# Logits of eight units at a time, one key scaling moved to VectorE, and the last unit's logits with its result as the stationary operand

## The chip, the cores and the metric

One core of one Trainium2 chip runs the whole program as one launch. The metric is device time in microseconds (us), the median of a few runs. The engines are named as in the profile: PE is TensorE (PEld its weight load), DVE is VectorE, ACT is ScalarE, POOL is GpSimd, SP is the engine that issues most of the loads and stores.

## The reference

First comes a gated linear attention, token by token, for 4 batches of 8 heads, 768 tokens, head size 48:

```
state = alpha[:, :, t, :, None] * state + einsum('bhd,bhe->bhde', k[:, :, t], v[:, :, t])
y[:, :, t] = einsum('bhd,bhde->bhe', q[:, :, t], state)
```

Its output, seen as 3072 rows of 384 channels, goes through a mixture of 8 experts. The logits are `x @ w_gate`. All 24,576 pairs of token and expert are gone through in order of falling logit; a token goes to the first expert that has fewer than 384 tokens so far. Each expert then computes `relu(x @ w1) @ w2` on its 384 tokens.

## The kernel before

**Attention.** The work is cut into 24 units, n = 0 to 23: unit n is 128 tokens (chunk n // 4) of batch n % 4, with all 8 heads. For each unit, `unit(n)` records these steps:
- DVE: a backward scan of the decay, `sc` (line 449), a reciprocal (451), a forward scan `ga` (454), and, for 18 of the units, the key scaling `kh` (459).
- POOL: the query scaling `qh` (464), the causal mask on the scores `sm` (502, two halves), and for the units in `K_POOL` the key scaling instead of DVE.
- PE: keys turned (485), scores `s` (495), states (510), and the result `y`, first the part carried from the state, then the part within the chunk (both 541).
- ACT: copies of these out of the PSUM, among them `yta` (564), the unit's result, channels on the partitions.
- DVE: the new state `st` (526), for units 0 to 19 from the second chunk on.

**Logits.** `logits(g, ns)` computes a group of units in `LOGITS`. PE multiplies the gate weights (stationary, 32 columns per unit) with the units' results (574). A unit's logits stand in one of four partition blocks, so four units fill a tile. ACT copies the tile (600), PE turns it (585), and DVE copies it into the table `L` (591). The last unit has a group of its own: four partial products side by side (582), which DVE sums (589) after the same copy and turn.

**Choice and routing.** When the first 20 units' logits are in `L`, DVE computes their digit tables (`choice(0, ...)`); the last four units follow in `choice(1, ...)`, which starts with the maximum on line 621. Then a search over digits alternates between DVE compares (935) and PE counts (906, 882) and gives the token list of the first expert. The attention result must stand in DRAM by then, tokens on the rows, since the tokens are gathered from there: each unit is turned by PE (four pieces, line 692 or 701), copied by ACT and stored by SP (710). `Y_EARLY` = 4 units are turned during attention, units 4 to `Y_IN_ATTENTION` - 1 at its end, the rest between the steps of the search.

**Experts.** 8 experts of 30 us follow, nearly all PE. Constants for the routing (line 331 to 413) are made on POOL between the attention's steps.

**What sets the order.** Every step is recorded by `op(...)` with an engine, an estimated duration, what it reads and writes, and a due time `at`. `plan()` simulates the engines and emits the instructions of each engine in the order that results; each engine then runs its own list in order. So a change of one step can move others on every engine. `banks` names PSUM areas that two engines shall not use at the same moment: the logits' tile and the states' tile share the areas `T` and `KX`.

Of the kernel before, what the change touches and what calls it, by code (L numbers as in the profile page):

```python
# [15 lines left out]
WARM_UP = 10  # L16
Y_IN_ATTENTION, Y_EARLY, EARLY_AT = 10, 4, 3.0
CUTS, CUTS_L = (0, 16, 24), (0, 12, 20, 24)
SAME, CHOICE, AHEAD_S = 0.8, 23.15, 0.8
LOGITS = ((0, 4), (4, 8), (8, 12), (12, 16), (16, 20), (20, 23), (23, 24))  # L20
CONST_AT, CONST_STEP, FILLS, FILL_END = 2.5, 0.5, 80, 6
FIRST_DMA = (dict(al=-0.4, k=0.87, q=1.35, v=0.5), dict(al=0.66, k=1.02, q=0.68, v=0.65))
WG_AT, Q_DVE, K0_AT = -1.4, (), 0.05
K_FIRST = ()
K_ELSE, K_POOL, M_ACT = 0, {n: 4 for n in (2, 6, 10, 14, 18, 22, 23)}, range(4, 23)
F0, TE = 26.0, 30.5
# [11 lines left out]
AF = mybir.ActivationFunctionType  # L38
OP = mybir.AluOpType
# [3 lines left out]
def gla_moe_kernel(ctx, tc, q, k, v, alpha, w_gate, w12, out):  # L43
    nc = tc.nc
    C = 128
    NC = 6
    H = 8
    HP = H // 2
    NU = q.shape[0]
# [4 lines left out]
    E = w_gate.shape[1]  # L54
# [103 lines left out]
    def ring(name, n, shape, dtype=F32):  # L158
        return [ap_.tile(shape, dtype, name=f"{name}{i}") for i in range(n)]
# [13 lines left out]
    ST = ring("st", NBAT, [128, HP, D])  # L173
    LT = ring("lt", RING["lt"], [128, C])
    YT = [YTA[:, n].rearrange("p (h s t) -> p h s t", h=2, s=2) for n in range(NU)]
# [11 lines left out]
    kvp = kx[:, KT:KT + HP * D].rearrange("p (u d) -> p u d", d=D)  # L187
    ltp = XB[:, KT:KT + C]
    lgp = XB[:, KT + C:KT + 2 * C].rearrange("p (n e) -> p n e", e=32)
    fcp = kx[:, KT + HP * D:KT + HP * D + E]  # L190
# [378 lines left out]
    def logits(g, ns):  # L569
        def some(n0, n1):  # L570
            for j in range(HP):
                for n in range(n0, n1):
                    u = n - ns[0]
                    P_.matmul(ltp[32 * u:32 * u + 32], wg[:, j], YT[n][:, j % 2, j // 2], start=j == 0,
                              stop=j == HP - 1, skip_group_check=True)

        one = len(ns) == 1
        lt_, lg_ = (yps[:, 0, :C], yps[:, 1, :C].rearrange("p (n e) -> p n e", e=32)) if one else (ltp, lgp)

        def single():  # L580
            for j in range(HP):
                P_.matmul(lt_[32 * j:32 * j + 32], wg[:, j], YT[ns[0]][:, j % 2, j // 2], start=True, stop=True)

        def turned():
            P_.transpose(lg_.rearrange("p n e -> p (n e)"), lt, ident)

        def out_():
            if len(ns) == 1:
                V.tensor_reduce(L[:, ns[0]], lg_[:, :, :E].rearrange("p j e -> p e j"), axis=X_, op=OP.add)
            else:  # L590
                V.tensor_copy(L[:, ns[0]:ns[-1] + 1], lgp[:, :len(ns), :E])

        lt = LT[g % RING["lt"]]
        at = ns[-1]
        t_, g_ = (("Y0",), ("Y1",)) if one else (("T", "KX"),) * 2
        LT_ = "LT1" if one else "LT"
        op("PE", 0.33 if one else 0.9, single if one else lambda: some(ns[0], ns[-1] + 1), shape=32,
           r=[("yt", n) for n in ns] + [("wg", 0)], w=[(LT_, g)], banks=t_, at=at + 1.0,
           after=lastw["yt", NU - 2] if one else ())
        op("ACT", 0.3, lambda: A.activation(lt, lt_, AF.Copy), r=[(LT_, g)], w=[("lt", g)], banks=t_, at=at + 1.0)  # L600
        op("PE", 0.12, turned, shape=128, r=[("lt", g)], w=[("LG", g)], banks=g_, at=at + 1.1,
           after=() if one else lg_read[-1:])
        lg_read.append(op("DVE", 0.18, out_, r=[("LG", g)], banks=g_, at=ns[-1] + 1.1, after=copied[-1:]))
        copied.append(lg_read[-1])

# [811 lines left out]
```

## Time and profile before

| | us |
|---|---|
| median of 3 runs (lowest, highest) | 370.01 (369.34, 370.06) |
| the profiled execution, whole | 369.01 |
| its span, first to last instruction | 367.4 |
| PE busy | 350.3 (95%) |
| DVE busy | 267.0 (73%) |
| ACT busy | 185.8 (51%) |
| POOL busy | 177.9 (48%) |

The granted clock of PE is 0.991 of full speed over the span. The shares are means over stages with different limits: POOL is idle for long in the experts' part and nearly full in attention. Attention takes the first 97 us, the search and the first gather the next 20, the experts the rest.

### The profile page before, as it was taken

The numbers are of one execution on the slowest core, as the hardware profiler recorded it, in microseconds if no ns is written. First come the engines' busy times: TensorE is split into PE (matmuls) and PEld (weight loads), VectorE is DVE, ScalarE is ACT, GpSimd is POOL, SyncE is SP. The second block draws the span as 40 slices with busy tenths as digits, with TensorE's granted clock in tenths as the row PEclk, the third lists the DMA queues.
The fourth block names the chain that finished last, engine by engine and source line by source line (L and its number), as shares of the span: only waits on it lengthen the run. The fifth ranks groups of instructions, "written<-read, shape, count | busy, mean of one in ns | idle before, by whom it ended". The sixth has DMA issues, their size and how long they took to land.

```text
span 367.4 us, 9669 instructions
## 1 busy us (share of the span) xinstructions
PE 350.3 (95%) x3710; PEld 310.8 (85%) x3710; DVE 267.0 (73%) x741; ACT 185.8 (51%) x387; POOL 177.9 (48%) x298
## 2 busy tenths in 40 slices
PE   8989999999999999899999999999999999999990
PEld 4778888887776779789899989889989999999990
DVE  7999999998878998888978978878777733131110
ACT  4697888886551741651552553543462474343120
POOL 2898999999402312351524625603722862304021
PEclk9999999999999999999999999999999999999996
DMA  7999998840176956999799699698898899986001
GB/s 232 368 351 377 394 300 265 272 131 2 45 249 221 324 105 167 306 173 271 245 218 260 206 243 237 206 272 165 277 266 171 297 337 239 287 201 127 24 22 43
DMA packets 28782, 81.71 MB, mean 222 GB/s; under 512 B 3904, under 2 KB 10304, under 8 KB 28736
## 3 DMA queue, kind: packets, MB, share of 16 engines
q0 software_dynamic: 11024, 52.70, 54.2%
q1 hardware_dynamic: 17712, 28.39, 22.7%
q8 instruction: 29, 0.48, 0.5%
q14 instruction: 17, 0.14, 0.1%
HBM read 71.64 MB, written 9.44 MB: 221 GB/s over the span
## 4 chain that ended last, share of the span: by engine, by line
PE 61%; DVE 19%; issue 9%; DMA 3%; POOL 3%; SPq 1%; ACT 1%; POOLq 0%; DVEq 0%; ACTq 0%
PE h L1283 21%; PE y L1315 21%; PE y L541 3%; DVE sc L449 3%; PE xt L882 3%; PE s L495 2%; DVE ga L454 2%; PE h L1135 2%; DVE kh L459 2%; DVE wset L1190 2%; DMA al<-in_alpha_dram 2%; DVE cmp L935 1%; DMA vr<-in_v_dram 1%; POOL out_dram L1335 1%; DVE xl L1259 1%
## 5 line engine op out<-in xcount | busy, mean ns | idle before, releaser
L1315 PE MATMUL y<-wset,hh 128*128 128x384 f32 x384 | 101.7, 342 | 0.0
L1283 PE MATMUL h<-xh,wset 128*128 128x384 f32 x384 | 93.4, 345 | 0.3 <-DVE hl L1298 0.3
L1296 ACT ACTIVATE hh<-h 128x384 fp32r<-128x384 f32 x64 | 31.3, 490 | 93.7 <-PE h L1283 84.3
L1315 PEld LDWEIGHTS y<-wset,hh 128*128 128x128 f32 x384 | 69.2, 188 | 1.0 <-issue 1.0
L1283 PEld LDWEIGHTS h<-xh,wset 128*128 128x128 f32 x384 | 68.1, 188 | 0.8 <-DVE hl L1298 0.6
L1315 PE MATMUL y<-wset,hl 128*128 128x384 f32 x192 | 65.9, 343 | 0.0
L1298 DVE SCALAR_TENSOR_TENSOR hl<-h,hh 128x384 fp32r<-128x384 f32 x64 | 35.3, 554 | 39.6 <-ACT hh L1296 38.9
L1208 POOL DMA_DIRECT2D wset<-in_w_dram x23 | 20.9, 909 | 63.9 <-ACT wset L1204 63.8
L1283 PE MATMUL h<-xl,wset 128*128 128x384 f32 x192 | 47.3, 345 | 0.0
L1335 POOL DMA_INDIRECT out_dram<-yo,idx x24 | 24.9, 1039 | 41.3 <-ACT yo L1326 37.4
L1204 ACT ACTIVATE wset<-wset 128x768 fp32r<-128x768 f32 x46 | 36.6, 840 | 12.6 <-DMA wset<-in_w_dram 12.2
L1125 POOL DMA_INDIRECT xr<-x_dram,idx x24 | 25.4, 1060 | 23.5 <-DVE idx L1121 9.0
L1315 PEld LDWEIGHTS y<-wset,hl 128*128 128x128 f32 x192 | 36.1, 188 | 0.5 <-issue 0.4
L1283 PEld LDWEIGHTS h<-xl,wset 128*128 128x128 f32 x192 | 34.1, 188 | 0.9 <-issue 0.7
L502 POOL TENSOR_SCALAR_AFFINE_SELECT sm<-sm 128x512 f32<-128x512 f32 x48 | 32.2, 693 | 3.2 <-ACT sm L500 2.9
L464 POOL TENSOR_TENSOR qh<-qr,ga 128x512 f32<-128x512 f32 (+1 forms) x25 | 29.8, 1193 | 5.3 <-DVE ga L454 4.3
L454 DVE TENSOR_TENSOR_SCAN ga<-al,d 128x516 f32<-128x516 f32 (+1 forms) x25 | 29.6, 1183 | 1.8
L449 DVE TENSOR_TENSOR_SCAN sc<-al,d 128x516 f32<-128x516 f32 (+1 forms) x25 | 29.3, 1173 | 1.3 <-DMA al<-in_alpha_dram 1.2
L500 ACT ACTIVATE sm<-s 128x512 f32<-128x512 f32 x48 | 26.1, 595 | 7.3 <-PE s L495 6.8
L495 PE MATMUL s<-qh,kh 64*128 64x128 f32 x384 | 27.4, 282 | 1.0 <-POOL qh L464 1.0
L495 PEld LDWEIGHTS s<-qh,kh 64*128 64x128 f32 x384 | 23.6, 189 | 2.4 <-POOL qh L464 2.1
L1178 POOL DMA_DIRECT2D raw<-in_w_dram x9 | 5.2, 580 | 41.4 <-DVE bk L1098 19.0
(218 smaller groups left out, 590.7 us busy)
## 6 DMA issues: line engine op xcount, KB each, us to landing
wset<-in_w_dram POOLq DMA_DIRECT2D x46, 768.0 KB
raw<-in_w_dram POOLq DMA_DIRECT2D x9, 768.0 KB
qr<-in_q_dram SPq DMA_DIRECT2D x24, 256.0 KB, 4.7
kr<-in_k_dram SPq DMA_DIRECT2D x24, 256.0 KB, 4.8
al<-in_alpha_dram SPq DMA_DIRECT2D x23, 258.5 KB, 4.7
vr<-in_v_dram SPq DMA_DIRECT2D x24, 192.0 KB, 4.6
x_dram<-xga SPq DMA_DIRECT2D x8, 384.0 KB, 2.7
x_dram<-xga SPq DMA_DIRECT2D x8, 192.0 KB, 3.3
```

The costliest lines, as they stand in the source:

```text
L449: V.tensor_tensor_scan(sc[:, lo + 1:hi + 1][:, ::-1], a[:, lo + 1:hi + 1][:, ::-1], dps[:, FO + lo:FO + hi][:, ::-1], 1.0, op0=OP.mult, op ...
L454: V.tensor_tensor_scan(ga[:, lo:hi], a[:, lo:hi], dps[:, lo:hi], 1.0, op0=OP.mult, op1=OP.add)
L464: (V if n in Q_DVE else G).tensor_mul(qh[:, ps_], qr[:, ps_], ga[:, lo:hi].rearrange("p (g x) -> p g x", x=C1)[:, :, 1:])
L495: P_.matmul(sps[h][:, p], kh[hs, p], qh[hs, p], start=True, stop=True)
L500: op("ACT", 0.6, lambda h=h: A.activation(sm[:, h], sps[h], AF.Copy), r=[(f"S{h}", n)], w=[("sm", n)], banks=(f"S{h}",), at=n + 0.4)
L502: op("POOL", 0.65, lambda h=h: G.affine_select(sm[:, h], sm[:, h], pattern=[[0, HP], [1, C]], compare_op=OP.is_ge, fill=0.0, base=0, chann ...
L1204: pre.append(op("ACT", 0.84, lambda hs=hs: A.activation(WS[i % 2][:, 1, g][:, hs], WS[i % 2][:, 0, g][:, hs].bitcast(F32), AF.Copy, scale= ...
L1283: P_.matmul(o(), WS[i % 2][:, a, g, c0 + d * 128:c0 + (d + 1) * 128], x[:, d], start=m_ == 0 and d == 0, stop=m_ == 2 and d == DB - 1)
L1296: a_ = op("ACT", 0.49, lambda: A.activation(HHT[m], o(), AF.Relu), after=[y], r=[("hb", n_)], w=[("hh", n_)], at=at, boost=25, lat=0.1)
L1298: op("DVE", 0.474, lambda: V.scalar_tensor_tensor(HLT[m], o(), 0.0, HHT[m], op0=OP.max, op1=OP.subtract), after=[a_], r=[("hb", n_), ("hh" ...
L1315: P_.matmul(YB[b][:, :Dm], a[:, bs], w, start=q == 0 and n == 0, stop=q == FB - 1 and n == 2)
L1335: st_ = nc.gpsimd.indirect_dma_start(out=out, out_offset=bass.IndirectOffsetOnAxis(ap=IDX[i][:, b:b + 1], axis=0), in_=YO[c % 5], in_offse ...
```

## The change

The groups of logits become (0, 4), (4, 12), (12, 20), (20, 23), (23, 24). A group of eight units is computed as two blocks of four in one PE step; ACT copies both blocks with one instruction, PE turns them with two transposes, DVE copies both with one instruction. The group's first step now waits for the DVE copy of the group ahead of it.

The last unit's logits have the unit's result as stationary operand and the gate weights, 8 columns, as moving one. They come out with the tokens on the partitions, summed over the four channel blocks in the PSUM, and DVE copies them straight into `L`; the ACT copy, the turn and the sum go.

Unit 22 leaves `K_POOL`, so its key scaling is a DVE instruction. `Y_IN_ATTENTION` is 9, so 5 units and not 6 are turned at the end of attention, and 15 and not 14 during the search.

```diff
-Y_IN_ATTENTION, Y_EARLY, EARLY_AT = 10, 4, 3.0
+Y_IN_ATTENTION, Y_EARLY, EARLY_AT = 9, 4, 3.0
-LOGITS = ((0, 4), (4, 8), (8, 12), (12, 16), (16, 20), (20, 23), (23, 24))
+LOGITS = ((0, 4), (4, 12), (12, 20), (20, 23), (23, 24))
-K_ELSE, K_POOL, M_ACT = 0, {n: 4 for n in (2, 6, 10, 14, 18, 22, 23)}, range(4, 23)
+K_ELSE, K_POOL, M_ACT = 0, {n: 4 for n in (2, 6, 10, 14, 18, 23)}, range(4, 23)
-    LT = ring("lt", RING["lt"], [128, C])
+    LT = ring("lt", RING["lt"], [128, 2, C])
-    ltp = XB[:, KT:KT + C]
-    lgp = XB[:, KT + C:KT + 2 * C].rearrange("p (n e) -> p n e", e=32)
+    ltp = XB[:, KT:KT + 2 * C]
+    lgp = ltp.rearrange("p (n e) -> p n e", e=32)
...
         def some(n0, n1):
-            for j in range(HP):
-                for n in range(n0, n1):
-                    u = n - ns[0]
-                    P_.matmul(ltp[32 * u:32 * u + 32], wg[:, j], YT[n][:, j % 2, j // 2], start=j == 0,
-                              stop=j == HP - 1, skip_group_check=True)
+            for a in range(n0, n1, 4):
+                for j in range(HP):
+                    for n in range(a, min(a + 4, n1)):
+                        u = n - a
+                        P_.matmul(ltp[32 * u:32 * u + 32, (a - n0) // 4 * C:(a - n0) // 4 * C + C], wg[:, j],
+                                  YT[n][:, j % 2, j // 2], start=j == 0, stop=j == HP - 1, skip_group_check=True)
...
         def single():
             for j in range(HP):
-                P_.matmul(lt_[32 * j:32 * j + 32], wg[:, j], YT[ns[0]][:, j % 2, j // 2], start=True, stop=True)
+                P_.matmul(lg_, YT[ns[0]][:, j % 2, j // 2], wg[:, j, :E], start=j == 0, stop=j == HP - 1)
...
         def turned():
-            P_.transpose(lg_.rearrange("p n e -> p (n e)"), lt, ident)
+            for a in range(0, len(ns), 4):
+                P_.transpose(lg_[:, a:a + 4].rearrange("p n e -> p (n e)"), lt[:, a // 4], ident)
...
             if len(ns) == 1:
-                V.tensor_reduce(L[:, ns[0]], lg_[:, :, :E].rearrange("p j e -> p e j"), axis=X_, op=OP.add)
+                V.tensor_copy(L[:, ns[0]], lg_)
...
+        if one:
+            op("PE", 0.6, single, shape=128, r=[("yt", ns[0]), ("wg", 0)], w=[("LG1", g)], banks=("Y1",), at=at + 1.0,
+               after=lastw["yt", NU - 2])
+        else:
+            op("PE", 0.45 + 0.45 * two, lambda: some(ns[0], ns[-1] + 1), shape=32, r=[("yt", n) for n in ns] + [("wg", 0)],
+               w=[("LT", g)], banks=t_, at=at + 1.0, after=lg_read[-1:])
+            op("ACT", 0.2 + 0.1 * two, lambda: A.activation(lt[:, :two], lt_.rearrange("p (a t) -> p a t", t=C), AF.Copy),
+               r=[("LT", g)], w=[("lt", g)], banks=t_, at=at + 1.0)
+            op("PE", 0.12 * two, turned, shape=128, r=[("lt", g)], w=[("LG", g)], banks=t_, at=at + 1.1)
```

The order of the instructions moves at more places than the diff shows. On PE, in the last units of attention: before, the scores of unit 21 (`s`, from `qh0`) are followed by the logits of units 16 to 19 (16 matmuls) and the result of unit 20 (from `ms2` and `sm0`).

```order
L495 MATMUL s1_179<-qh0_161,kh0_158 128x128
L574 MATMUL xx_181<-yta_121,wg_69 32x128 x16
L541 MATMUL y_180<-qh2_163,ms2_170 48x128 x8
L541 MATMUL y_180<-sm0_166,vr2_149 48x128 x8
L585 MATMUL xx_181<-ident_63,lt0_175 128x128
L495 MATMUL s0_178<-qh1_162,kh1_159 128x128
```

The same place in the changed kernel, with the logits of units 12 to 19:

```order
L495 MATMUL s1_179<-qh0_161,kh0_158 128x128
L575 MATMUL xx_181<-yta_121,wg_69 32x128 x32
L541 MATMUL y_180<-qh2_163,ms2_170 48x128 x8
L541 MATMUL y_180<-sm0_166,vr2_149 48x128 x8
L587 MATMUL xx_181<-ident_63,lt0_175 128x128 x2
L495 MATMUL s0_178<-qh1_162,kh1_159 128x128
```

So 16 matmuls that stood four units earlier, ahead of the result of unit 16, and one transpose now stand behind the scores of unit 21. The groups (4, 8) and (8, 12) are joined in the same way at the later one's place, ahead of the scores of unit 13.

On POOL, from the query scaling of unit 20 (`qh2<-qr0`) on; `shifts_b`, `masks_b`, `scale` and `oneb4`, `oneb5` are constants for the routing. Before:

```order
L464 TENSOR_TENSOR qh2_163<-qr0_142,ga0_156 128x512
L407 MEMSET shifts_b_106 128x24
L408 MEMSET masks_b_107 128x24
L410 MEMSET scale_82 128x24
L375 MEMSET oneb5_93 128x128
L376 MEMSET oneb5_93 32x128
L502 AFFINE_SELECT sm1_167<-sm1_167 128x512 x2
L464 TENSOR_TENSOR qh0_161<-qr1_143,ga1_157 128x512
L459 TENSOR_TENSOR kh1_159<-kr2_139,sc1_154 128x512
L502 AFFINE_SELECT sm0_166<-sm0_166 128x512 x2
L464 TENSOR_TENSOR qh1_162<-qr2_144,ga0_156 128x512
```

The same stretch in the changed kernel, from the row behind the query scaling of unit 20 on:

```order
L502 AFFINE_SELECT sm1_167<-sm1_167 128x512 x2
L375 MEMSET oneb4_92 128x128
L376 MEMSET oneb4_92 32x128
L378 MEMSET oneb4_92 1x128
L407 MEMSET shifts_b_106 128x24
L408 MEMSET masks_b_107 128x24
L410 MEMSET scale_82 128x24
L464 TENSOR_TENSOR qh0_161<-qr1_143,ga1_157 128x512
L502 AFFINE_SELECT sm0_166<-sm0_166 128x512 x2
L375 MEMSET oneb5_93 128x128
L376 MEMSET oneb5_93 32x128
L464 TENSOR_TENSOR qh1_162<-qr2_144,ga0_156 128x512
```

The mask of a unit (`sm`) now follows a query scaling directly, with the constants behind it, here and at most other units; the constants `oneb5` stand behind the query scaling of unit 21 (`qh0<-qr1`), and the key scaling of unit 22 (`kh1`) is gone.

On DVE, from the state of unit 18 (`st2<-ms0`) to the scans of unit 22 and 23. Before:

```order
L526 TENSOR_TENSOR st2_173<-ms0_168,xx_181 128x192
L459 TENSOR_TENSOR kh0_158<-kr1_138,sc0_153 128x512
L449 SCALAR_TENSOR_TENSOR sc1_154<-al2_134,d_177 128x516
L451 RECIPROCAL d_177<-sc1_154 128x4
L526 TENSOR_TENSOR st3_174<-ms1_169,xx_181 128x192
L454 SCALAR_TENSOR_TENSOR ga0_156<-al2_134,d_177 128x516
L449 SCALAR_TENSOR_TENSOR sc2_155<-al3_135,d_177 128x516
```

The same stretch in the changed kernel:

```order
L526 TENSOR_TENSOR st2_173<-ms0_168,xx_181 128x192
L454 SCALAR_TENSOR_TENSOR ga1_157<-al1_133,d_177 128x516
L526 TENSOR_TENSOR st3_174<-ms1_169,xx_181 128x192
L459 TENSOR_TENSOR kh0_158<-kr1_138,sc0_153 128x512
L449 SCALAR_TENSOR_TENSOR sc1_154<-al2_134,d_177 128x516
L451 RECIPROCAL d_177<-sc1_154 128x4
L459 TENSOR_TENSOR kh1_159<-kr2_139,sc1_154 128x512
L454 SCALAR_TENSOR_TENSOR ga0_156<-al2_134,d_177 128x516
L449 SCALAR_TENSOR_TENSOR sc2_155<-al3_135,d_177 128x516
```

The key scaling of unit 22 (`kh1`) stands between the two scans of its unit, and the states of units 18 and 19 stand one place earlier, that of unit 19 ahead of the key scaling of unit 21 (`kh0`).

## Rows read from the trace of the kernel before

**Rows 1.** Busy time by stage: PE, PEld, DVE, ACT, POOL with (instructions), then PEclk, DMA share, GB/s
```profile
35.00:93.00 58.00, 57.34 (x1228) 49.02 (x1216) 53.75 (x74) 47.24 (x124) 56.34 (x114) 1.00 0.69 228
...
117.40:367.40 250.00, 237.81 (x1680) 219.82 (x1677) 162.31 (x551) 103.54 (x179) 91.74 (x126) 0.99 0.80 212
```

**Rows 2.** Waits of POOL from 35 to 93 us: us in total, times, longest
```profile
POOL qh L464 <- DVE st L526: 1.1, 1, 1.1
```

**Rows 3.** Waits of DVE from 46 to 88 us: us in total, times, longest
```profile
DVE st L526 <- PE xx L574: 1.0, 2, 0.6
```

**Rows 4.** Timeline of PE, 56 to 61 us: start us, us, instruction, count
```profile
56.42 1.12 PE L495 MATMUL s<-qh,kh 64*128 64x128 f32 x16
57.48 1.08 PE L574 MATMUL xx<-yta,wg 128*32 128x128 f32 x32
58.49 0.66 PE L541 MATMUL y<-qh,ms 48*48 48x128 f32 x16
59.07 1.08 PE L541 MATMUL y<-sm,vr 128*48 128x128 f32 x16
60.09 0.33 PE L585 MATMUL xx<-ident,lt 128*128 128x128 f32 x1
60.34 0.56 PE L510 MATMUL xx<-vr,kn 128*48 128x48 f32 x16
60.84 0.45 PE L485 MATMUL xx<-ident,kh 48*128 48x48 f32 x8
```

**Rows 5.** Timeline of PE, the scores of units 21 and 23; [idle before, releaser]
```profile
85.12 1.16 PE L495 MATMUL s<-qh,kh 64*128 64x128 f32 x16
...
92.04 1.16 PE L495 MATMUL s<-qh,kh 64*128 64x128 f32 x16 [0.21 <-POOL qh L464]
```

**Rows 6.** Timeline of POOL, 52 to 86 us
```profile
52.02 1.77 POOL L502 TENSOR_SCALAR_AFFINE_SELECT sm<-sm 128x512 f32<-128x512 f32 x2
...
58.41 1.17 POOL L464 TENSOR_TENSOR qh<-qr,ga 128x512 f32<-128x512 f32 x1
59.54 1.67 POOL L502 TENSOR_SCALAR_AFFINE_SELECT sm<-sm 128x512 f32<-128x512 f32 x2
...
74.55 1.67 POOL L502 TENSOR_SCALAR_AFFINE_SELECT sm<-sm 128x512 f32<-128x512 f32 x2
...
78.16 0.22 POOL L375 MEMSET oneb<- 128x128 bf16 x1
...
82.28 0.20 POOL L375 MEMSET oneb<- 128x128 bf16 x1
...
82.70 1.21 POOL L502 TENSOR_SCALAR_AFFINE_SELECT sm<-sm 128x512 f32<-128x512 f32 x2
83.89 1.17 POOL L464 TENSOR_TENSOR qh<-qr,ga 128x512 f32<-128x512 f32 x1
85.03 1.17 POOL L459 TENSOR_TENSOR kh<-kr,sc 128x512 f32<-128x512 f32 x1
```

**Rows 7.** Timeline of DVE, two key scalings
```profile
58.97 1.17 DVE L459 TENSOR_TENSOR kh<-kr,sc 128x512 f32<-128x512 f32 x1
...
78.09 0.69 DVE L459 TENSOR_TENSOR kh<-kr,sc 128x512 f32<-128x512 f32 x1
```

**Rows 8.** Chain that ended last, 96 to 100 us: start us, us, what
```profile
96.39 1.00 PE xx L574 x24
...
97.40 0.43 PE y L582 x8
...
98.67 0.12 PE y L585
...
98.81 0.20 DVE L L589
...
99.04 0.20 DVE m L621
```

**Rows 9.** Timeline of PE, units turned between the search's steps
```profile
102.31 1.37 PE L692 MATMUL turned<-ident,yta 112*128 112x112 f32 x12
```

More of the change, by code (lines that the diff above doesn't have):

```diff
@@ L570, in some @@
         def some(n0, n1):
-            for j in range(HP):
-                for n in range(n0, n1):
-                    u = n - ns[0]
-                    P_.matmul(ltp[32 * u:32 * u + 32], wg[:, j], YT[n][:, j % 2, j // 2], start=j == 0,
-                              stop=j == HP - 1, skip_group_check=True)
-        one = len(ns) == 1
-        lt_, lg_ = (yps[:, 0, :C], yps[:, 1, :C].rearrange("p (n e) -> p n e", e=32)) if one else (ltp, lgp)
+            for a in range(n0, n1, 4):
[4 more added lines that the diff above has]
+                                  YT[n][:, j % 2, j // 2], start=j == 0, stop=j == HP - 1, skip_group_check=True)
+        one, two = len(ns) == 1, 1 + (len(ns) > 4)
+        lt_, lg_ = ltp[:, :C * two], yps[:, 1, :E] if one else lgp
         def single():
             for j in range(HP):
-                P_.matmul(lt_[32 * j:32 * j + 32], wg[:, j], YT[ns[0]][:, j % 2, j // 2], start=True, stop=True)
+                P_.matmul(lg_, YT[ns[0]][:, j % 2, j // 2], wg[:, j, :E], start=j == 0, stop=j == HP - 1)
         def turned():
-            P_.transpose(lg_.rearrange("p n e -> p (n e)"), lt, ident)
+            for a in range(0, len(ns), 4):
+                P_.transpose(lg_[:, a:a + 4].rearrange("p n e -> p (n e)"), lt[:, a // 4], ident)
         def out_():
             if len(ns) == 1:
-                V.tensor_reduce(L[:, ns[0]], lg_[:, :, :E].rearrange("p j e -> p e j"), axis=X_, op=OP.add)
+                V.tensor_copy(L[:, ns[0]], lg_)
             else:
@@ L594, in logits @@
         at = ns[-1]
[L595 to L603, printed above, removed]
+        t_ = ("T", "KX")
+        if one:
[7 more added lines that the diff above has]
+            op("PE", 0.12 * two, turned, shape=128, r=[("lt", g)], w=[("LG", g)], banks=t_, at=at + 1.1)
+        lg_read.append(op("DVE", 0.18, out_, r=[("LG1" if one else "LG", g)], banks=("Y1",) if one else t_, at=ns[-1] + 1.1, after=copied[-1:]))
         copied.append(lg_read[-1])
```

## The prediction

> **What bounds the kernel now.** I read the busy time by stage first. In the experts' part, from 117.4 us on, PE is busy for 237.8 of 250 us [rows 1]; the change touches nothing there, so it can only start that part earlier or later. In attention three engines are full at once: from 35 to 93 us PE is busy for 57.3, POOL for 56.3 and DVE for 53.8 of 58 us [rows 1]. The waits say which of them leads. POOL waits once in these 58 us, for 1.1 us, early in the stretch [rows 2]: after that it works through its list without a gap, so each thing on the list moves everything behind it. DVE waits twice for the PE's logits, 1.0 us in all [rows 3]: it has that much to spare. At the end PE takes the scores of unit 21 at 85.12, just behind POOL's query scaling of that unit (83.89 + 1.17 = 85.06), and those of unit 23 at 92.04 after a wait of 0.21 for POOL [rows 5, 6]. So from 85.12 on PE runs nearly without a gap to the last logits (the chain has them from 96.39), and behind these a chain of small steps leads to the maximum at 99.04, with which the routing begins [rows 8]. The end of attention is therefore: when POOL delivers unit 21's queries, plus PE's work behind that, plus the chain to 99.04. All behind it is the search and the experts and moves with it.
>
> **The price of joined logits.** One group costs PE 58.49 - 57.48 = 1.01 us for 16 matmuls (32 pieces in the profile) and 60.34 - 60.09 = 0.25 us for its turn [rows 4]. A group of eight costs twice the first, and for its second turn what one costs on the chain, 0.12 us [rows 8]. The two joins thus save 2 x 0.13 us of PE time, 0.3 us, and with the change-overs they spare (the 0.33 us that the lone turn is shown with, against 0.12) up to 0.7. But this is not where the end is decided. The second join takes the block of units 12 to 15 from a place four units earlier and puts it behind the scores of unit 21, where every microsecond of PE counts: + 1.01 + 0.12 = **+1.13 us**, if the scores of unit 21 start when they did. Its bounds are 0.9 (the change-over spared) and 1.3 (the second turn at 0.25).
>
> What PE saves ahead of unit 21 helps only if POOL is earlier as well.
>
> **POOL ahead of unit 21.** Two constants, `oneb5`, now stand behind the query scaling of unit 21: 82.70 - 82.28 = 0.42 us less ahead of it [rows 6]. Unit 22's key scaling on POOL, 1.17 us, stood behind it (85.03), so its going doesn't reach this point; it only takes away the 0.21 us of wait at unit 23. What remains is how often POOL is held up by DVE. A DVE key scaling that begins at 58.97, while POOL scales queries until 59.58, takes 1.17 us, and the mask that follows on POOL takes 1.67 in place of 1.21 [rows 6, 7]: the two take turns, and POOL loses about 0.46. The one at 78.09, beside a POOL memset, takes 0.69 [rows 6, 7], and POOL loses nothing. Of the ten masks of units 10 to 19, five took 1.56 to 1.77 and one 1.34 (the first of the slow ones at 52.02, the last at 74.55): 2.3 us lost to eight key scalings on DVE. In the changed list the constants no longer stand between query scaling and mask, and a ninth key scaling (unit 22) can reach DVE before POOL is through with unit 21's queries. At the same mean loss, 2.3 / 8 = 0.29, the ninth adds 0.29; I take +0.25, so POOL's part is -0.42 + 0.25 = **-0.17 us**. Bounds: all nine meet a query scaling or a mask, 9 x 0.46 = 4.1, +1.8 on before, which gives +1.4; or only three do, 1.4, -0.9 on before, which gives -1.3.
>
> The Trainium skill (SBUF — State Buffer, "Who interferes with whom") says that a VectorE instruction with two SBUF inputs contends with a GpSimd instruction that reads the SBUF, but not with one that only writes it, and that the loser blocks fully. The rows agree: queries and mask collide, memsets don't. By it the order of the POOL list is a price of its own, and it speaks against this change; the first rival is what it would do here.
>
> **DVE.** Unit 22's key scaling adds 0.69 to 1.17 us [rows 7] ahead of the last three scans, whose last feeds unit 23's queries on POOL. Its cover is PE: the scores of unit 23 come 1.13 us of added PE work later than before, and POOL has lost 1.17 us of work ahead of them. I cost it at 0; without that cover it would cost the 0.69. The joined copy into `L` waits for both blocks, ACT's copy and both turns, and behind it in DVE's list stand the state of unit 12 and the scan of unit 16. At this very place DVE waited 0.6 us for the logits already [rows 3], so I cost this at 0 too; the other 0.4 us of wait goes with the early group. The state of unit 19 now stands ahead of unit 21's keys and waits for PE's states of that unit; the keys of unit 21 are needed only with its queries, so this is in the POOL bounds.
>
> **The last unit.** Before: its four products from 97.40 (0.43), the turn ending 98.79, the sum at 98.81, the maximum at 99.04 [rows 8]. The new form starts at the same event, the copy of unit 23's result. No row shows a product with 8 moving columns and 128 stationary ones. From below, 0.3 (less than the 0.43 of now); from above, 8 pieces at the 0.12 of the turn, 0.96. I take 4 x 0.12 = 0.48, near to what the old form takes. Then 97.88, the group's turn 0.12, two copies at 0.20 each, as the sum now takes, and 0.07 of hand-over: the maximum at 98.47, **-0.57 us** (bounds -0.75 and -0.1).
>
> **One unit more in the search.** Four turns, 1.37 / 3 = 0.46 us [rows 9]. They stand where PE waits for DVE's compares or spins; if all were on the path +0.46, if the shorter list in front of the search (four turns fewer) helps, -0.1. I take **+0.05**.
>
> **The sum.** 1.13 - 0.17 - 0.57 + 0.05 = +0.44 us. The profiled execution takes 369.01 (its span 367.4 and 1.6 around it), so 369.45; the median of the runs shown lies 1.0 higher at 370.01, so I forecast **370.4 us**. A measurement of this kernel can tell about 0.2%, 0.74 us, from no change: this is no change that can be told. The forecast's own range, with POOL between -0.8 and +0.1, is 369.8 to 370.7.
>
> **First rival: POOL is held up more often (slower).** Place: POOL's list from unit 10 to 21. In the new list a mask follows a query scaling directly at eight units, where before constants often lay between. A DVE key scaling that comes up while the queries run then always hits the mask. When I follow the two lists by the durations above, seven of the nine collide: 7 x 0.46 = 3.2 us, +0.9 on before. With the 0.42 that left, unit 21's queries come 0.5 late; the end is 1.13 + 0.5 - 0.57 + 0.05 = +1.1, **371.1 us**. It decides from a little over six collisions on (the sum then passes 0.74). For it: three of the slow masks, 59.54 among them, follow a query scaling directly. Against: DVE's place against POOL shifts with every step, and a key scaling that comes up late in a mask falls into the constants and costs nothing.
>
> **Second rival: PE becomes the bound ahead of unit 21 (faster).** If only three key scalings collide, POOL is 1.3 us earlier at unit 21 and the end is 1.13 - 1.3 - 0.57 + 0.05 = -0.7; with the 0.7 us that the joins can save in full and the waits for POOL gone, -1.1, **368.9 us**. For it: PE has a whole group less to do ahead of that point, and the constants behind the masks are a shelter. Against: POOL showed no gap, and every mask it must deliver is the same.
>
> A third way, that the last unit's products take 0.96 us or more, would leave 0.1 of the 0.57 and give 370.9; it is in the ranges.
>
> **Chances.** Forecast 0.41, first rival 0.34, second 0.25. The range must take in most of both rivals and the loose end of the last unit: 368.7 to 371.8 us. From the same cases: faster by over 0.2% 0.25, within 0.41, slower 0.34.
>
> **What the profile after would show.** Right: POOL again without gaps up to unit 21's queries; their end within 0.8 us of 85.06; from there to the last logits some 12.4 us of PE where it was 11.3 (96.39 - 85.12); then 2.1 us to the maximum where it was 2.65. The first rival shows as seven or more masks or scalings of POOL lengthened by 0.4 to 0.6. The second shows as PE without a wait for POOL and unit 21's scores before 84 us. I am wrong if the 12.4 us don't appear, that is, if something other than PE's own work ends the last units; or if a stall shows that no row here has, most of all a DVE wait in front of the joined copy or of unit 19's state that delays unit 21's keys.

## The result, and the profile after

The changed kernel takes 374.06 us (median of 4 runs, 373.46 to 374.37) against 370.03 us (369.34 to 370.08), a ratio of 1.011 [1.0086, 1.0134]: slower. A second set of runs of the same kernel gave 373.85 us against 371.07, 1.0066 [1.0031, 1.0101], so the loss is some 2.5 to 4 us. The profiled execution took 373.93 us, its span 372.3.

The windows of the changed kernel (as [rows 1], the second stretch begun 2.5 us later, since the search ends later) show the same amount of work among the experts: PE is busy for 238.22 us where it was 237.81. Ahead of 93 us PE has lost 2.1 us of busy time:

```profile
35.00:93.00 58.00, 55.22 (x1192) 47.65 (x1184) 52.22 (x75) 45.38 (x120) 56.08 (x111) 1.00 0.69 225
119.90:372.30 252.40, 238.22 (x1680) 219.90 (x1677) 162.85 (x551) 103.18 (x179) 93.65 (x126) 0.99 0.79 210
```

Its waits, of POOL from 35 to 93 us, of PE from 35 to 99 and of DVE from 46 to 93 (as [rows 2, 3]):

```profile
POOL qh L464 <- DVE ga L454: 0.5, 1, 0.5
...
PE s L495 <- POOL qh L464: 2.2, 3, 1.3
PE d L541 <- POOL sm L502: 0.5, 1, 0.5
...
DVE L L593 <- PE xx L587: 2.4, 1, 2.4
DVE st L526 <- PE xx L510: 0.9, 1, 0.9
```

POOL still works nearly without a gap, but now PE waits for it (2.2 us for queries, before 0.2). DVE waits longer for the turned logits (2.4 us, before 1.0, at 89 us and so outside [rows 3]) and anew for PE's states (0.9 us). The timeline of PE places them (answers to [rows 5, 8]; L575 is the logits' line now, L583 the last unit's, L587 the turns):

```profile
82.47 1.16 PE L495 MATMUL s<-qh,kh 64*128 64x128 f32 x16
...
86.57 1.16 PE L495 MATMUL s<-qh,kh 64*128 64x128 f32 x16 [1.34 <-POOL qh L464]
87.67 1.96 PE L575 MATMUL xx<-yta,wg 128*32 128x128 f32 x64
...
91.15 0.44 PE L587 MATMUL xx<-ident,lt 128*128 128x128 f32 x2
91.52 1.16 PE L495 MATMUL s<-qh,kh 64*128 64x128 f32 x16
...
97.92 1.23 PE L541 MATMUL d<-sm,vr 128*48 128x128 f32 x16 [0.53 <-POOL sm L502]
99.09 1.07 PE L575 MATMUL xx<-yta,wg 128*32 128x128 f32 x24
100.09 1.06 PE L583 MATMUL y<-wg,yta 128*128 128x8 f32 x8
```

Three things are to be seen. Unit 21's scores come at 86.57 (before 85.12; 0.51 us of this is a later start of the execution, since unit 9's scores, ahead of all that the change moves, stand at 42.06 and 41.55). PE stood idle for 1.34 us ahead of them: the time that it saved by the missing group of units 12 to 15 went into its waits for POOL. The joined block behind them takes 1.96 us. And ahead of unit 23's last products PE waits 0.53 us for a mask, which no row of before has. The last logits start at 99.09 instead of 96.32.

The timeline of POOL (as [rows 6]) says why the queries are late, and the mask:

```profile
74.26 1.63 POOL L464 TENSOR_TENSOR qh<-qr,ga 128x512 f32<-128x512 f32 x1
75.85 1.22 POOL L502 TENSOR_SCALAR_AFFINE_SELECT sm<-sm 128x512 f32<-128x512 f32 x2
77.89 1.33 POOL L464 TENSOR_TENSOR qh<-qr,ga 128x512 f32<-128x512 f32 x1
...
82.36 1.68 POOL L502 TENSOR_SCALAR_AFFINE_SELECT sm<-sm 128x512 f32<-128x512 f32 x2
84.92 1.60 POOL L464 TENSOR_TENSOR qh<-qr,ga 128x512 f32<-128x512 f32 x1
...
96.12 2.33 POOL L502 TENSOR_SCALAR_AFFINE_SELECT sm<-sm 128x512 f32<-128x512 f32 x2 [0.96 <-ACT sm L500]
```

From 47 us to unit 21's queries nine of POOL's masks and scalings are lengthened, 3.6 us in all over their undisturbed 1.22 and 1.18; in before it was six, 2.4 us. Up to 75 us the count is six in both; the three new ones are those at 77.89, 82.36 and 84.92. Each lies beside a key scaling on DVE, and unit 23's mask beside the search's first large compare (timeline of DVE, as [rows 7]):

```profile
77.52 0.67 DVE L459 TENSOR_TENSOR kh<-kr,sc 128x512 f32<-128x512 f32 x1
...
82.44 0.35 DVE L526 TENSOR_TENSOR st<-ms,xx 128x192 f32<-128x192 f32 x1 [0.94 <-PE xx L510]
82.71 0.84 DVE L459 TENSOR_TENSOR kh<-kr,sc 128x512 f32<-128x512 f32 x1
84.82 0.67 DVE L459 TENSOR_TENSOR kh<-kr,sc 128x512 f32<-128x512 f32 x1
91.69 0.22 DVE L593 COPY L<-xx 128x64 f32<-128x64 f32 x1 [2.40 <-PE xx L587]
...
95.89 1.48 DVE L655 TENSOR_TENSOR cmp<-dig,iota 128x2560 bf16<-128x2560 bf16 x1
```

82.71 is unit 21's keys, 84.82 unit 22's (the ninth scaling on DVE). The state of unit 19, at 82.44, stands ahead of unit 21's keys and waits 0.94 us for PE.

### The profile page after: what moved, and what is told of

Its sections match the earlier page's. It is cut to its first block, busy times and chain, and to the rows that moved or that the text cites. A ratio compares the mean times of both kernels' runs of the same rounds, so it can differ in the third digit from the quotient of the medians.

```text
span 372.3 us, 9637 instructions
## 1 busy us (share of the span) xinstructions
PE 350.7 (94%) x3703; PEld 311.8 (84%) x3703; DVE 265.3 (71%) x740; ACT 184.9 (50%) x384; POOL 181.8 (49%) x297
## 4 chain that ended last, share of the span: by engine, by line
PE 37%; DVE 17%; issue 15%; POOL 12%; DMA 12%; ACT 2%; POOLq 1%; SPq 0%; DVEq 0%; ACTq 0%
PE h L1287 13%; PE y L1319 12%; DMA wset<-in_w_dram 6%; DVE sc L449 4%; DMA raw<-in_w_dram 3%; POOL qh L464 3%; POOL xr L1129 3%; DMA kr<-in_k_dram 2%; POOL sm L502 2%; PE y L541 2%; DVE kh L459 2%; DVE ga L454 2%; POOL out_dram L1339 2%; PE s L495 1%; PE xt L886 1%
## 5 line engine op out<-in xcount | busy, mean ns | idle before, releaser
L1129 POOL DMA_INDIRECT xr<-x_dram,idx x24 | 27.2, 1134 | 23.3 <-DVE idx L1125 8.7
L502 POOL TENSOR_SCALAR_AFFINE_SELECT sm<-sm 128x512 f32<-128x512 f32 x48 | 33.5, 721 | 4.8 <-ACT sm L500 4.8
L464 POOL TENSOR_TENSOR qh<-qr,ga 128x512 f32<-128x512 f32 (+1 forms) x25 | 31.6, 1264 | 4.9 <-DMA qr<-in_q_dram 4.4
```

The source lines that it names most:

```text
L464: (V if n in Q_DVE else G).tensor_mul(qh[:, ps_], qr[:, ps_], ga[:, lo:hi].rearrange("p (g x) -> p g x", x=C1)[:, :, 1:])
L502: op("POOL", 0.65, lambda h=h: G.affine_select(sm[:, h], sm[:, h], pattern=[[0, HP], [1, C]], compare_op=OP.is_ge, fill=0.0, base=0, chann ...
L1129: gathers[i, b] = op("POOL", 1.3, lambda b=b: nc.gpsimd.indirect_dma_start(out=XR[r2][:, b], out_offset=None, in_=x_dram, in_offset=bass.I ...
```

## The experiments

**One part at a time, on the kernel before.** Four kernels, each with one part of the change. What the diffs leave unnamed is as before.

```
p_joins   LOGITS = ((0,4),(4,12),(12,20),(20,23),(23,24)) and the joined form of logits()
p_k22     K_POOL without unit 22
p_single  the last unit's logits with its result as stationary operand
p_turn9   Y_IN_ATTENTION = 9
```

Expected of p_joins: 

> The kernel before with the joined groups of logits alone (unit 22's keys on POOL, old form for the last unit, 6 units turned at the end). Theory: the joins are the loss. They put 16 matmuls behind the scores of unit 21 (1.0 us, and 0.12 for the turn) and they put POOL's masks right behind its query scalings, where DVE's key scalings hold them up. Then the scores of unit 21 start 0.8 to 1.6 us later than the 85.12 of before, the maximum that opens the routing comes 2.0 to 3.0 us after 99.04, and the time is 2.0 to 4.0 us over before. Rival: the loss comes from unit 22's keys on DVE, which delay the last scans and hit POOL's queries; then this kernel is within 0.7 us of before. Second rival: it comes from the new form of the last unit; then the same.

Expected of p_k22: 

> The kernel before with unit 22's key scaling on DVE alone. Theory (the joins are the loss): POOL has 1.17 us less behind the queries of unit 21, PE's wait of 0.21 us for the scores of unit 23 goes; time -0.5 to +0.3 us. Rival (this part is the loss): the key scaling stands ahead of the last scans and collides with POOL's queries; scores of unit 22 or 23 wait 0.5 us or more, time +1 us or more.

Expected of p_single: 

> The kernel before with the last unit's logits in the new form alone (its result stationary, gate weights moving). Theory: the products take 0.9 to 1.06 us where the old ones take 0.43, and the copy, the turn and the sum that go make up for it: the step from the last logits of the group of three to the first maximum stays at 2.5 to 2.65 us; time -0.3 to +0.2 us. Rival: the new products are the loss, +0.7 us or more.

Expected of p_turn9: 

> The kernel before with one unit fewer turned at the end of attention (5 and not 6) and so 15 in the search. Theory: PE turns it in time it would else spend on fillers or waiting for DVE; the first gather and all behind it move by -0.2 to +0.2 us. Rival: the last unit's copy and store come later than the token list, and the gather waits for them: +0.5 us or more at the first turn of the gathered rows (120.94 before).

Measured against 370.65 us: p_joins 374.49, 1.0085 [1.005, 1.012]; p_k22 371.15, 1.0015 [0.9989, 1.004]; p_single 370.88, 1.0019 [0.999, 1.0048]; p_turn9 371.54, 1.0028 [1.0008, 1.0048]. The joins are the loss. But p_joins does not lose where its theory had it: with the starts set alike, unit 21's scores come 0.4 us later than before and the maximum 1.3 (expected 0.8 to 1.6, and 2.0 to 3.0). To the first gathered rows it is 1.7 us, and the profile doesn't place the rest of the 3.2 us [1.9, 4.4]. In p_single the new form of the last unit wins next to nothing: from the last logits to the maximum it is 2.62 us, before 2.72; the search behind it took 22.48 us (before 21.90), for which I have no cause. In p_turn9 the search from the maximum (99.17) to the first gathered rows turned on PE (121.06) takes 21.89 us, before 21.90, so the tenth unit costs nothing in its own place; 0.28% of its time I can't place.

In p_k22 the theory missed too: PE's wait of 0.21 us at unit 23 doesn't go, it grows to 0.78 (DVE, and below the dots PE):

```profile
84.09 2.53 DVE L459 TENSOR_TENSOR kh<-kr,sc 128x512 f32<-128x512 f32 x1
...
92.67 1.16 PE L495 MATMUL s<-qh,kh 64*128 64x128 f32 x16 [0.78 <-POOL qh L464]
```

Unit 22's key scaling began while POOL scaled unit 21's queries (83.73 to 84.90) and came through only behind the mask that followed them directly, at 86.07; the last scans and unit 23's queries are late by it. With the starts set alike the maximum comes 0.65 us later, which the time can neither show nor exclude (-0.4 to +1.5 us).

**Which join.** The changed kernel with one join undone, with both undone, and as it is.

```
a_late_apart   (4, 12), (12, 16), (16, 20)
a_early_apart  (4, 8), (8, 12), (12, 20)
a_groups4      (4, 8), (8, 12), (12, 16), (16, 20)
a_again        (4, 12), (12, 20): the changed kernel
```

Expected of a_late_apart: 

> The changed kernel with units 12 to 15 and 16 to 19 as two groups of four again; units 4 to 11 stay joined. Theory (the late block costs its own PE time behind unit 21, the collisions on POOL come with the earlier join): from the start of unit 21's scores to the last logits 11.3 us as before instead of 12.5, queries of unit 21 still late (85.7 to 86.3), masks lengthened ahead of it still 3.2 us or more: 372.5 to 373.1 us. Rival (the loss is all POOL's, PE has room behind unit 21): the last logits stay at 98.5 or later and the time at 373.5 to 374.3.

Expected of a_early_apart: 

> The changed kernel with units 4 to 7 and 8 to 11 as two groups of four again; units 12 to 19 stay joined. In it the constants of POOL stand between query scaling and mask as before, up to unit 18. Theory (masks that follow a query scaling directly take the collisions): masks and scalings lengthened ahead of unit 21's queries by 2.4 us in all, not 3.6, unit 21's scores at 85.3 or earlier, from there 12.4 us to the last logits: 372.6 to 373.2 us. Rival (where the constants stand does not matter): unit 21's scores at 86.3 or later, 373.5 to 374.3.

Expected of a_groups4: 

> The changed kernel with all groups of four as before; unit 22's keys on VectorE, the new form of the last unit and nine units turned ahead stay. Theory (the joins are nearly the whole loss): 370.3 to 371.5 us, within 0.4% of before, unit 21's scores at 85.0 to 85.4, 11.3 us to the last logits. Rival (the three small edits add up, +0.5, +0.2 and +0.9 us by their single runs): 371.5 to 372.0.

Expected of a_again: 

> The changed kernel itself, once more. Theory (POOL's collisions, the late block and the stalls among the experts belong to the kernel): 373.5 to 374.5 us; unit 21's scores behind POOL's queries again, more than 85.8 after the start's own offset is taken off, from the first scatter to the last 199.5 to 200.5 us. Rival (part of the 4 us is the single profiled execution's own): collisions ahead of unit 21 or the time from the first scatter to the last come out 1 us or more smaller at the same median.

Measured against 371.07 us: a_late_apart 370.53, 0.9978 [0.9947, 1.0009]; a_early_apart 376.27, 1.011 [1.002, 1.0199]; a_groups4 371.27, 1.0009 [0.9977, 1.0041]; a_again 373.85. Undoing the late join gives back the whole loss and more than its theory allowed; undoing the early one gives nothing. a_groups4 keeps p_k22's wait of 0.78 us at unit 23, and from unit 21's scores to the last logits it takes 11.85 us and not the 11.3 of its theory. The timeline of PE in a_late_apart:

```profile
82.82 1.16 PE L495 MATMUL s<-qh,kh 64*128 64x128 f32 x16
...
85.51 1.16 PE L495 MATMUL s<-qh,kh 64*128 64x128 f32 x16
86.60 1.08 PE L575 MATMUL xx<-yta,wg 128*32 128x128 f32 x32
...
96.15 1.07 PE L575 MATMUL xx<-yta,wg 128*32 128x128 f32 x24
```

PE doesn't wait for POOL at unit 21, and from there to the last logits it is 10.64 us, even less than in before (11.20); in a_again it is 98.43 - 85.92 = 12.51. In a_early_apart unit 21's scores come at 85.96 after 1.34 us of idle PE, and the last logits at 98.69: the theory's 85.3 fell. The constants on POOL stand as in before only up to unit 18 there; at units 19 and 20 its masks follow the queries directly, as in every kernel with the late join, and these two are lengthened by 0.46 us each, unit 21's queries by 0.18; in all it is 3.5 us where the theory had 2.4 (timeline of POOL in a_early_apart):

```profile
78.10 1.68 POOL L502 TENSOR_SCALAR_AFFINE_SELECT sm<-sm 128x512 f32<-128x512 f32 x2
...
81.74 1.69 POOL L502 TENSOR_SCALAR_AFFINE_SELECT sm<-sm 128x512 f32<-128x512 f32 x2
```

In before [rows 6] and in a_late_apart constants lie between query and mask at units 19 and 20, and the DVE scaling falls beside them. So the rival, that their place doesn't matter, isn't shown either: it matters at these two units, and at the units before, the collision only changes its partner (six up to 75 us in all kernels).

**The late join alone.** The kernel before with units 12 to 19 joined and nothing else.

```
b_late  LOGITS = ((0,4),(4,8),(8,12),(12,20),(20,23),(23,24)), all else as before
```

Expected: 

> The kernel before with one part of the change alone: units 12 to 15 and 16 to 19 joined; units 4 to 11 apart, unit 22's keys on POOL, old form of the last unit, ten units turned ahead. Theory (this join is the whole loss): 373.4 to 375 us, 0.7 to 1.1% above before, unit 21's scores behind POOL with a wait of 0.9 or more on PE, 12.2 us or more from there to the last logits. Rival (it takes both joins): within 0.4% of before.

Measured: 373.58 us against 371.28, 1.0065 [1.0038, 1.0092]. Unit 21's scores at 85.85 wait 1.16 us for POOL, and the last logits follow 12.31 us later, at 98.16. This one join is the loss. On POOL eight masks are lengthened, 3.2 us in all, and the two that before has not are again those that follow the queries of units 19 and 20 directly (POOL, and below the dots PE):

```profile
78.20 1.68 POOL L502 TENSOR_SCALAR_AFFINE_SELECT sm<-sm 128x512 f32<-128x512 f32 x2
...
81.83 1.68 POOL L502 TENSOR_SCALAR_AFFINE_SELECT sm<-sm 128x512 f32<-128x512 f32 x2
...
85.85 1.16 PE L495 MATMUL s<-qh,kh 64*128 64x128 f32 x16 [1.16 <-POOL qh L464]
```

Unit 23's mask is nearly free here (1.30 us at 95.88, with the compare behind it at 96.61): the join loses as much without the stall that the changed kernel has there. Its search takes 22.36 us, 0.5 longer than b_again's 21.85, for which I have no cause. Since the join also moves POOL's list, the later block and the new order of POOL come together in every one of these kernels; the join with POOL's old order was not run.

**POOL's collisions.** The changed kernel with the keys of units 20 and 21 scaled on DVE for the first pair of heads of four; the other three pairs are left out.

```
-   op("DVE", ..., lambda p0=p0, pm=pm: scale_k(V, p0, pm), ...
+   op("DVE", ..., lambda p0=p0, pm=1 if n in (20, 21) else pm: scale_k(V, p0, pm), ...
```

Expected of a_keys_short: 

> The changed kernel, in the same order on every engine, with the VectorE key scalings of units 20 and 21 done for the first of four pairs only (the other three are left out; their keys are those of older units). Theory (these two scalings hold up POOL's mask of unit 19 and its queries of unit 21, 0.45 us each, at the point that sets the end): both at their undisturbed 1.22 and 1.18 us, unit 21's scores and all behind 0.8 us earlier (85.1 for 85.9), 372.9 to 373.3 us. Rival (POOL is late for other reasons, or the time is PE's): unit 21's scores at 85.7 or later, 373.6 us or more.

Measured: 373.49 us against 371.0, 1.0061 [1.0032, 1.009]. Unit 21's scores come at 85.40 where a_again has 85.92. The mask of unit 19 is free, but the queries of unit 21 are not (POOL, and below the dots DVE, in a_keys_short):

```profile
81.58 1.28 POOL L502 TENSOR_SCALAR_AFFINE_SELECT sm<-sm 128x512 f32<-128x512 f32 x2
...
83.75 1.60 POOL L464 TENSOR_TENSOR qh<-qr,ga 128x512 f32<-128x512 f32 x1
...
83.64 0.68 DVE L459 TENSOR_TENSOR kh<-kr,sc 128x512 f32<-128x512 f32 x1
```

The scaling at 83.64 is that of unit 22, which I had taken for unit 21's: the edit took away two of the three new collisions, and the end moved by 0.52 us in the trace. That these collisions delay unit 21 is shown by the trace: in four executions of the unshortened list its scores come 44.35 to 44.51 us behind unit 9's, here 43.82. The time can't show half a microsecond. The theory's 0.8 us was for a pair that I had named wrongly.

**Unit 23's mask.** Is it the search's compare of 128x2560 that stretches it? Two edits of the changed kernel.

```
a_cmp_late   the compare planned with unit 23's mask as predecessor
a_cmp_after  the compare planned behind the last unit's own compare: CM["op"].pre.add(x)
```

Expected of a_cmp_late: 

> The changed kernel with the search's first large compare on VectorE held back until the mask of unit 23 is through; nothing else moved. Theory (the compare holds that mask on POOL, 2.33 us for 1.27, and PE waits 0.53 for it): the mask takes 1.2 to 1.3 us, PE's wait is gone, the last logits come 0.4 to 0.6 earlier, and the time is 373.3 to 373.6 us. Rival (the compare's own lateness costs the search as much): the last logits earlier, but the first gathered turn not, 373.8 to 374.3 us.

Expected of a_cmp_after: 

> The changed kernel with the search's first large compare (128x2560) placed on VectorE behind the last unit's steps, so that it runs some 6 us later, when unit 23's mask is long through. The order up to there is the same. Theory (the compare holds that mask on POOL): the mask takes 1.25 to 1.35 us instead of 2.33, PE does not wait for it, and from unit 21's scores to the last logits it is 12.0 us instead of 12.5; behind it the compare stands in the search's way by 1.0 to 1.5 us, so the time is 374.4 to 375.2. Rival (something else stretches the mask): mask still 2.3, from unit 21's scores to the last logits still 12.5.

a_cmp_late told nothing: a predecessor on another engine only orders the plan, VectorE's list stayed as it was, and the compare started at 95.42, ahead of the mask's 95.65; with 374.27 us it is one more set of runs of the changed kernel. In a_cmp_after the compare starts at 102.51, and the mask is free (POOL, and below the dots PE):

```profile
96.01 1.22 POOL L502 TENSOR_SCALAR_AFFINE_SELECT sm<-sm 128x512 f32<-128x512 f32 x2 [0.96 <-ACT sm L500]
...
86.46 1.16 PE L495 MATMUL s<-qh,kh 64*128 64x128 f32 x16 [1.34 <-POOL qh L464]
...
97.11 1.04 PE L541 MATMUL d<-sm,vr 128*48 128x128 f32 x16
98.08 1.07 PE L575 MATMUL xx<-yta,wg 128*32 128x128 f32 x24
```

From unit 21's scores to the last logits it is 11.62 us instead of 12.51: the compare's hold on the mask cost 0.89, more than PE's wait of 0.53 shows: in a_again the products behind it start 1.61 us after those ahead of them, here 0.91, and take 1.23 us for 1.04. Of the 0.89 only 0.60 reaches the maximum: here the last unit's products wait 0.22 us for ACT's copy, and from the last logits to the maximum it is 2.84 us and not 2.55. Its time, 375.0 us (1.0103 [1.0054, 1.0153]), is as expected with the compare in the search's way.

**Do the experts lose too?** From the first gathered rows to the last scatter the profile of before has 238.77 us, that of after 241.05. Either a later start costs the experts more than its length, or the one execution was short.

```
b_delay   before + 6 reductions of 128x160 on VectorE ahead of the last maximum
b_delay2  before + 12 of them
b_again   before
```

Expected of b_delay: 

> The kernel before with six small reductions, 0.35 us each, put on VectorE ahead of the last maximum, so that the search and the experts start 2.1 us later and nothing else changes. Theory (experts move with the end of attention, one for one): first gathered turn 2.0 to 2.2 us later, time 2.0 to 2.2 us above before. Rival (a later start costs the experts more, since their weights then come later against the work that wants them): the same first gathered turn, but 2.8 to 3.6 us above before, with PE waiting 1 us more behind 250 us.

Expected of b_delay2: 

> The kernel before with twelve small reductions on VectorE ahead of the last maximum in place of the six of the earlier run: the search and the experts start 4.0 us later by the 1.92 that the six took, doubled (0.34 each). Theory (one for one): 3.8 to 4.4 us above before. Rival (each microsecond of delay costs the experts another half): 5.5 us or more above before.

Expected of b_again: 

> The kernel before itself, once more, for a second profile of its experts. Theory (its first profiled execution, 1.0 to 2.0 us under the medians of its runs, had lucky weights): from the first gathered turn to the last scatter 239.7 to 240.7 us instead of 238.8, PE waiting 3.8 to 5 us behind 120 us, not 3.05. Rival (238.8 is the kernel's own, the later kernels lose among the experts): 238.6 to 239.2.

Measured: b_delay 374.01 us against 371.0, 1.0074 [1.0047, 1.0101], 1.7 to 3.7 us for a delay of 1.92, which holds both theories. b_delay2 376.24 against 371.28, 1.0118 [1.0085, 1.0151], 4.4 us [3.2, 5.6] for a maximum 4.04 us late: one for one, as far as the interval tells. b_again 371.48. First gathered rows and last scatter of b_again, from its timelines of PE and POOL:

```profile
121.09 0.52 PE L1244 MATMUL xt<-ident,xr 128*128 128x128 f32 x3 [0.21 <-issue]
...
362.77 0.96 POOL L1335 DMA_INDIRECT out_dram<-yo,idx  x1 [1.24 <-DVE yo L1329]
```

and of a_again:

```profile
122.94 0.52 PE L1248 MATMUL xt<-ident,xr 128*128 128x128 f32 x3 [0.43 <-DMA xr<-x_dram,idx]
...
364.36 0.96 POOL L1339 DMA_INDIRECT out_dram<-yo,idx  x1 [1.24 <-DVE yo L1333]
```

That is 241.68 us for before and 241.42 for the changed kernel. The profile that I predicted from was an execution short in this part, and between these two the experts lose nothing. That they never lose is not shown: this stage took 238.8 to 242.3 us (mean 240.5) in the eleven profiled executions of kernels without the late join, and 240.7 to 243.3 (mean 241.7) in the eight with it. Some 1 us may be lost there as well.

**A better version?** The changed kernel without its late join, twice, and with ten units turned ahead (b_early).

```
b_early        (4, 12), (12, 16), (16, 20); Y_IN_ATTENTION = 10
a_late_apart2  as a_late_apart
```

Expected of b_early: 

> The changed kernel with units 12 to 15 and 16 to 19 apart again and ten units turned ahead as before: units 4 to 11 joined, unit 22's keys on VectorE and the new form of the last unit stay. Theory (the early join saves PE a change of group ahead of unit 21 and costs nothing, the tenth unit turned in attention is worth 0.3 to 0.9): 369.5 to 370.4 us, 0.1 to 0.4% under before. Rival (nothing left to gain, as POOL sets unit 21): within 0.1% of before.

Expected of a_late_apart2: 

> The changed kernel with units 12 to 15 and 16 to 19 apart, once more, in more rounds: does it beat the kernel before, as its first 0.9978 [0.9947, 1.0009] hints? Theory (its trace has the last maximum at 98.7, 0.3 to 0.5 earlier than the two profiles of before): 0.1% under before, 370.4 to 371.0 us, interval with 1 in it or just below. Rival (no gain): 371.0 us or more.

Measured: b_early 371.7 us against 371.0, 1.0022 [0.9995, 1.005]; a_late_apart2 369.43 against 370.08, 0.9976 [0.9953, 1.0]. Twice 0.2% under before, with an interval that just touches 1: the changed kernel without its late join is at least as good as before and probably better by that much. b_early, one unit turned ahead more, met neither its theory nor its rival and doesn't bear out the cost of the ninth seen in p_turn9; what that unit is worth stays open at 0.3% either way.

## Why the prediction was wrong

It forecast 370.4 us, no change. I set a_again against b_again, two executions with like experts; unit 9's scores, ahead of all that the change moves, stand at 41.56 and 41.79, so a_again started 0.23 earlier.

- **Base.** 369.01 was low for this kernel, as b_again shows; the median I went by, 370.01, was met by later sets at 370.08 to 371.28. The ratio isn't touched by this.
- **Joined block, +1.13: right.** 1.96 for 1.08 us, and 0.44 for 0.33 for the turns: +0.99. In b_late, where the mask is nearly free, unit 21's scores to the last logits take 12.31 us where b_again has 11.22: +1.09. In the changed kernel the forecast 12.4 us came out at 12.51 by luck, from other parts: 10.64 (a_late_apart) + 0.99 + 0.89 for the mask.
- **POOL ahead of unit 21, -0.17: the step that failed, by 1.05 us.** Unit 21's scores come 85.92 - 85.27 + 0.23 = 0.88 later. This is the first rival: the collisions rose by 1.2 us, and `oneb5` gave 0.42 back. The rival counted seven of nine, and nine it was; it put its price at 0.5. Its reason, masks that follow queries directly, is borne out at units 19 and 20 in a_early_apart and b_late; in the changed kernel one of the new collisions is such a mask (82.36), the other two are queries. The third new collision is unit 22's key scaling, which I had priced at 0.25; it took 0.42. I had a bound that held it, +1.4, and chose the value near the mean loss.
- **DVE at 0: failed too.** I looked for a wait that something is queued behind, and only at the early joined copy; [rows 3] end at 88 us, ahead of the late one. That copy did wait, 2.40 us where the single one waited 1.04, but what it cost is another thing: the search's compare started at 95.24 us, 0.23 ahead of unit 23's mask (a_again), and that cost 0.89. In before one of the steps behind the copy was itself held by POOL's list, which kept the compare at 96.49, behind the mask at 93.96; begun later, at 91.65 in a_again, the same step took 0.59 us (DVE, before):

```profile
89.76 4.06 DVE L624 TENSOR_TENSOR val<-L,m 128x160 bf16<-128x160 f32 x1
...
96.49 1.48 DVE L651 TENSOR_TENSOR cmp<-dig,iota 128x2560 bf16<-128x2560 bf16 x1
```

  The mask's stall is the one "that no row here has"; no case of mine contained it. Unit 22's keys at 0 is right only with cover, as I wrote: in p_k22, without it, a stall of the scaling makes PE's wait at unit 23 grow by 0.57, where I had named 0.69.
- **Last unit, -0.57: mis-sized.** From the last logits to the maximum 2.55 us against 2.75, -0.20. The eight pieces took 0.99 on the chain, just over the upper bound (0.96) and not near the 0.48 that I took, for which I had counted four products and not their eight pieces; the forecast of 370.9 for this case had it right by itself.
- **A unit more in the search, +0.05:** 21.96 against 21.85 us, +0.11.

The rest of the 12.51 us is a gain that I had put at nothing: -0.58 (10.64 against 11.22). About half of it lies ahead of unit 23's scores, where a wait of 0.22 us for POOL is gone, and half behind them, where the products of the last two units stand in another order. Unit 22's keys alone don't bring it: p_k22 and a_groups4 wait 0.78 us at unit 23. a_late_apart, with the early join, has constants on POOL behind unit 21's queries (85.20), and there DVE's scaling came through in 1.42 us instead of 2.53. Together: 0.88 + 0.99 + 0.89 - 0.58 - 0.20 + 0.11 = +2.09 us to the first gathered rows, where the prediction had +0.44. The runs give +2.45 [1.15, 3.75] for a_again and +2.4 for b_late; the first set's +4.0 [3.2, 5.0] lies higher, and I have no cause for the difference beyond the spread between sets and the loss among the experts that stays open. One sum of the prediction is unclear: the second rival's -1.1 doesn't follow from the terms it names (-0.7, 0.7 saved and the waits gone make some -1.6); that case didn't occur.

The Trainium skill (SBUF — State Buffer, "Who interferes with whom") adds to the rule that I weighed: "Issue order, not op shape, decides who blocks." The trace agrees (last section): the compare of 1.48 us, begun 0.23 us ahead of the mask, kept it for 1.1 us longer. I had used the rule for how often the two meet and not for which of them comes first.

## What to carry over

Where an engine works through its list without a gap and another waits for it, moving work that is "off the path" on a third engine still shifts when their instructions meet: list the instructions that block each other near the end of the stage, and ask of each which starts first after the change. A group joined later moves PE's work from a place where the time it frees turns into waiting to one where every microsecond counts. And profile the kernel before twice: one execution can be 3 us short in a stage that the change doesn't touch.

## What the hardware showed that I had not expected

- **Which of the two started first, by a tenth of a microsecond, decided who paid.** After: unit 22's scaling started at 84.82, 0.10 ahead of unit 21's queries on POOL; it took its free 0.67, the queries 1.60. In a_late_apart the queries started first and took their free time, and the scaling paid (POOL, then DVE). Behind those queries stood a memset. Where a mask follows them at once it goes either way: in p_k22 the scaling waited through the mask too (2.53 us), at 58.97 in before it came in ahead of most of it [rows 6, 7]; why is open:

```profile
84.08 1.19 POOL L464 TENSOR_TENSOR qh<-qr,ga 128x512 f32<-128x512 f32 x1
...
84.40 1.42 DVE L459 TENSOR_TENSOR kh<-kr,sc 128x512 f32<-128x512 f32 x1
```

- **Narrow products aren't cheap.** Four fp32 products with a 128x128 stationary operand and 8 moving columns took 1.06 us, 0.12 for each of the 8 pieces; the four with 32 stationary columns and 128 moving ones 0.43.
- **Behind a pause in the search the clock was lower.** In b_delay2 the twelve reductions left PE busy for 23.32 of the 27 us from 98 to 125, at a mean granted clock of 0.87; b_again had 25.82 and 1.00. PE was busy for 1.23 of the 3 us from 101 to 104 and for 1.73 of the next 3; from 107 to 110 the granted clock was 0.50, the lower of its two levels, 1.2 GHz (windows of b_again, then of b_delay2). From the maximum to the first gathered rows it took 22.48 us for 21.85; that the clock is the cause is not shown, since p_single took 22.48 at a clock of 1.00.

```profile
98.00:125.00 27.00, 25.82 (x278) 18.97 (x275) 21.86 (x81) 12.67 (x28) 5.21 (x7) 1.00 0.67 227
```

```profile
98.00:125.00 27.00, 23.32 (x241) 18.53 (x238) 21.23 (x84) 9.55 (x21) 2.63 (x4) 0.87 0.53 183
101.00:104.00 3.00, 1.23 (x12) 0.93 (x10) 2.69 (x11) 1.23 (x3) 0.00 (x0) 1.00 0.63 218
...
107.00:110.00 3.00, 3.00 (x39) 2.89 (x38) 2.14 (x6) 1.30 (x4) 0.00 (x0) 0.50 0.36 131
```
